# Lower words of the weights on GpSimd, finer first pieces, means in two products, and another order of two attention steps in an attention and gated-network kernel

## The chip, the core and the metric

The kernel runs on one core of a Trainium2 chip. The metric is device time in microseconds for one execution; of several runs the median is taken. A profile is one further execution with a trace. Engines are named as the profile does: PE is TensorE (PEld its weight loads), DVE is VectorE, ACT is ScalarE, POOL is GpSimd, SP is SyncE, which issues most transfers here.

## The reference

The inputs are q, k and v with 4 batches, 8 heads, 768 positions and 64 columns a head, all float32. Each position attends to a local window of positions nearer than 16 and to 24 summaries, one for each block of 32 positions. A summary key is the maximum of the block's keys, a summary value is the mean of its values.

```python
k_sum = k.reshape(B, H, nb, block, D).max(axis=3)
v_sum = v.reshape(B, H, nb, block, D).mean(axis=3)
scores_l = scale * np.matmul(q, k.transpose(0, 1, 3, 2))      # masked to |i - j| < 16
scores_s = scale * np.einsum('bhsd,bhnd->bhsn', q, k_sum) + np.log(block)
a = softmax(np.concatenate([scores_l_m, scores_s], axis=-1))
attn = np.matmul(a, np.concatenate([v, v_sum], axis=2))
x = attn.transpose(0, 2, 1, 3).reshape(3072, 512)
out = ((x @ w1) * (x @ w2) @ w3) @ w_out
```

w1 and w2 are 512x1024, w3 is 1024x1024 and w_out 1024x512. They arrive as 64-bit floating point numbers; the kernel reads each as two 32-bit words.

## The kernel before, in words

**Products.** Every float32 operand of the network is kept as a high and a low part, and one product of 128x128 by 128x512 is three matmuls: high by high, low by high, high by low (`products`, L111 to L113). `fold_weights` (L193) multiplies w3 by w_out into wp once, 64 products; `gate` (L419 on) makes (x w1)(x w2) for 128 rows of the hidden layer, and `project` (L444) multiplies by wp. `low` (L108, L109) makes a low part as source minus high part.

**Weights.** They come in pieces of 512 numbers a partition (512 KB each), in the order of `EARLY`, then the rest of w3, then w1 and w2. `start_loads` issues the transfers, at most AHEAD of them before use, into a ring of ten buffers that keys and value rows share, and after the load with a given index it also issues the other loads that `LOADS` lists under that index. `convert` (L152) makes one unit of one or two pieces: ScalarE turns the upper words into float32 bits but for the last three (L167); VectorE shifts these bits left by three (L175) and then ORs the top three bits of the lower word into each piece (L178); ScalarE rounds this to the high part (L188); VectorE subtracts for the low part (L109).

**Attention.** A step is one group of 512 tokens by one pair of heads; there are 24. A step's scores (`scores`, L310, 32 matmul instructions into two of four sc banks) are reduced with the mask on VectorE (L333), put through the exponential on ScalarE (L347), their sums inverted on GpSimd and VectorE (L352, L353), and normalized. Then come `transposes` (L366, two tp banks), `evacuate` (L375, copies to SBUF), `outputs` (L384, 32 matmul instructions) and `keep_x`, which splits x into high and low parts. Before a step, GpSimd copies the summary keys into the key tile (`gather`, L304) and the summary values into the value tile (`load_sums`, L285).

**Summary values of the first batch.** `mean_products` multiplies six blocks of value rows by a constant matrix (`mean_sb`, made on GpSimd at the very start) and puts the 24 means of all columns on 120 output rows; one ScalarE copy makes vs0.

**Order.** Two parts are written out by hand. In the first phase a loop counts ticks, t, about one piece each. In every tick it advances the conversions, does what `WORK` lists for t, advances the first eight steps, begins a step if t is in `FIRST`, and then puts out products until RATE more columns are given (LATER_RATE from tick FIRST[4] on); a product counts 1536 columns, and one whose weights are not yet converted ends the tick's share. The order of the SP and PE instructions is exactly this order. `first_pair` (L555) takes a step over several ticks: scores; reduce and half the exponentials; the other half and the sums; normalize, and, from tick FIRST[s+1] on, transposes; outputs. The letters of `NORMALIZE` and `SECOND` say for each of these steps whether ScalarE (A) or VectorE (V) normalizes and makes the second copy. The sums of the fold's rows 2 and 3 lie in the tp banks, so that the first transposes need these to be stored in wp (`store`, L209 to L212).

In the second phase (L683 on) sixteen steps are done in pairs between network products, and GpSimd normalizes them (L356). The PE order of one pass is: transposes of an earlier step, scores of a new one, transposes of the second earlier step, scores of the second new one, outputs of both earlier steps, then network products.

Of the kernel before, what the change touches and what calls it, by code (L numbers as in the profile page):

```python
# [30 lines left out]
FIRST = (15, 18, 20, 22, 27, 32, 37, 44)  # L31
# [4 lines left out]
    *(("wo", 0, 0), ("w3", 0, 0), ("wo", 0, 1), ("w3", 1, 0), ("wo", 1), ("w3", 2, 0), ("w3", 3, 0)),  # L36
    *(("w3", 0, 1), ("w3", 1, 1), ("wo", 2), ("w3", 2, 1), ("w3", 3, 1), ("wo", 3)),
# [10 lines left out]
NORMALIZE = "VAAAAAAA"  # L48
SECOND = "AAAVAVVA"
SOONER = 400  # L50
RING = 10
# [19 lines left out]
def attention_moe(ctx, tc, qG, kW, kT, vP, vW, vB, mask, w1, w2, w3T, wo, out):  # L71
# [24 lines left out]
    make_identity(nc, ident)  # L96
    mask_sb = const.tile([P, 3, KR], F32, name="mask_sb")


    mean_sb = sb.tile([P, S // P, P], F32, name="mean_sb", tag="v", bufs=2)  # L100
    nc.gpsimd.memset(mean_sb, 0.0)
    for i in range(P // BLOCK):
        for at in (CUT, CUT - 64):
            part = mean_sb.rearrange("p t n -> p (t n)")[i * BLOCK : (i + 1) * BLOCK, at + i :: P + P // BLOCK]
            nc.gpsimd.memset(part[:, : S // P], 1.0 / BLOCK)
# [22 lines left out]
    def weight(name, i, src, shape, part=None):  # L128

        n = src.shape[1] // 2  # L130
        parts = range(n // PIECE) if part is None else [part]
        units.append((name, i, shape, list(parts), len(todo) + len(parts) - 1))
        for k in parts:
            todo.append(src[:, 2 * k * PIECE : 2 * (k + 1) * PIECE])

    def start_loads(at_least):

        while todo or due_loads:
# [8 lines left out]
            nc.sync.dma_start(raw, todo.pop(0))  # L147
# [4 lines left out]
    def convert(name, i, shape, parts, last):  # L152


        n = len(parts) * PIECE
# [6 lines left out]
        for k in range(len(parts)):  # L162
            raw = loading.pop(0)
            working.append(raw)
            words = raw.rearrange("p (n t) -> p n t", t=2)
            low_words.append(words[:, :, 0])
            nc.scalar.activation(  # L167
                f[:, k * PIECE : (k + 1) * PIECE],
                words[:, :, 1].bitcast(F32),
                AF.Prelu,  # L170
                scale=2.0**-112,
                alpha=-(2.0**32),
            )
            yield
        nc.vector.tensor_scalar(out=bits, in0=bits, scalar1=3, scalar2=None, op0=ALU.logical_shift_left)  # L175
        for k, low_word in enumerate(low_words):
            some = bits[:, k * PIECE : (k + 1) * PIECE]
            nc.vector.scalar_tensor_tensor(  # L178
                out=some, in0=low_word, scalar=29, in1=some, op0=ALU.logical_shift_right, op1=ALU.bitwise_or
# [6 lines left out]
        at = parts[0] * PIECE  # L186
# [4 lines left out]
        have.update((name, i, part) for part in parts)  # L191

    def fold_weights(order):  # L193
        acc = {}
        for i, j in order:
            while not {("w3", i, j * P // PIECE), ("wo", j // 2, j % 2 * DO // PIECE)} <= have:
# [59 lines left out]

    def mean_products(tiles):
        po = ps.tile([P, 512], F32, name="means", tag="sc", bufs=4)
        for i in range(S // P):
            nc.tensor.matmul(  # L260
                po[:KR, :DM],
                lhsT=mean_sb[:, i, :KR],
                rhs=tiles[i // 2][:, i % 2],
                start=i == 0,
                stop=i == S // P - 1,
            )
        return po
# [90 lines left out]
    def normalize_alone(s, sm, mx):  # L358

        if NORMALIZE[s] == "A":  # L360
            for j in range(NI):
                nc.scalar.activation(sm[:, j], sm[:, j], AF.Copy, scale=mx[:, 2, j : j + 1])
        else:
            nc.vector.tensor_tensor(sm, sm, mx[:, 2].unsqueeze(2).broadcast_to([P, NI, KR]), ALU.mult)

    def transposes(sm):  # L366

        tp = [ps.tile([P, 512], F32, name="tp", bufs=2) for _ in range(2)]
# [43 lines left out]
    def gate(f, x, hs):  # L412
        acc = []
        for w in range(2):
# [6 lines left out]
            for c in range(NC):  # L421
                while (GATES[w], k, c * FQ // PIECE) not in have:
# [46 lines left out]
    def queue(name, i, part=None):  # L469
        src, shape = {"wo": (wo, (2, DO)), "w3": (w3T, (NJ, P)), "w1": (w1, (NC, FQ)), "w2": (w2, (NC, FQ))}[name]  # L470
        weight(name, i, src[i], shape, part)
# [305 lines left out]
```

## Time and profile before

| what | us |
|---|---|
| median of 3 runs (542.31 to 544.02) | 543.22 |
| the profiled execution's own time | 541.49 |
| its span, from the first instruction to the last | 539.7 |
| PE busy | 517.6 |
| DVE busy | 238.6 |
| ACT busy | 239.8 |
| POOL busy | 56.8 |

The mean granted TensorE clock of this execution is 0.993 of full speed. In the rows below, a line of the timeline gives start, duration, engine, source line, operation, output and inputs with shapes, count, and in brackets the engine's idle time before it with what ended that. A row of the groups gives the busy time, the mean duration in ns, and the idle time before. A window row gives the stretch and its length, then the busy time and count for PE, PEld, DVE, ACT and POOL, then the granted clock, the transfers' share and GB/s.

### The profile page before, as it was taken

How to read it: one execution, taken by the hardware profiler on the slowest of the kernel's cores; microseconds unless marked ns; L12 is line 12 of the kernel's file. 1: busy time of each engine (PE TensorE's matmuls, PEld its weight loads, DVE VectorE, ACT ScalarE, POOL GpSimd, SP SyncE). 2: the span in 40 equal slices, each digit the busy share in tenths (PEclk: the TensorE clock that was granted, in tenths of full speed). 3: DMA queues.
4: the chain of work that ended last, by engine and by line, in shares of the span. 5: the costliest groups of instructions: out<-in, count | busy, mean ns of one | idle time of the engine just before them, and what ended most of it. 6: DMA issues, size and time to landing. Idle time of an engine off the chain costs nothing.

```text
span 539.7 us, 9919 instructions
## 1 busy us (share of the span) xinstructions
PE 517.6 (96%) x3852; PEld 419.9 (78%) x3852; DVE 238.6 (44%) x686; ACT 239.8 (44%) x688; POOL 56.8 (11%) x103
## 2 busy tenths in 40 slices
PE   2897999999999999999999999999999999899997
PEld 1655777888788888888888888888888888788885
DVE  5879889998504227633253043251142350222210
ACT  5548998876436127126254153261172361222210
POOL 1010221110003001103002011021020020000000
PEclk9997999999999999999999999999999999999999
DMA  8999699775614005642050150050150020000001
GB/s 305 406 371 342 193 306 350 244 210 169 205 57 152 0 24 146 202 142 80 0 149 21 60 170 21 0 166 23 60 170 1 16 60 39 21 21 0 1 19 58
DMA packets 30574, 67.21 MB, mean 125 GB/s; under 512 B 4032, under 2 KB 7616, under 8 KB 30528
## 3 DMA queue, kind: packets, MB, share of 16 engines
q1 hardware_dynamic: 27072, 60.30, 34.7%
q10 hardware_dynamic: 3456, 6.29, 3.1%
q8 instruction: 30, 0.49, 0.4%
q14 instruction: 16, 0.13, 0.1%
HBM read 58.51 MB, written 6.29 MB: 120 GB/s over the span
## 4 chain that ended last, share of the span: by engine, by line
PE 91%; DVE 3%; ACT 3%; DMA 1%; issue 1%; POOL 0%; SPq 0%; POOLq 0%; ACTq 0%
PE mm L113 79%; PE po L393 5%; PE sc L319 4%; PE tp L373 3%; DVE w L109 1%; DMA wraw<-in_w3T_dram 1%; DVE wf L178 1%; ACT w L188 1%; PE means L260 1%; ACT sm L347 1%; DVE wf L175 1%; ACT wf L167 0%; ACT pt L378 0%; ACT wp L211 0%; DVE wp L109 0%
## 5 line engine op out<-in xcount | busy, mean ns | idle before, releaser
L113 PE MATMUL mm<-x,w 128*128 128x512 f32 x1152 | 265.1, 390 | 0.0
L113 PEld LDWEIGHTS mm<-x,w 128*128 128x128 f32 x1152 | 215.4, 188 | 45.8 <-issue 0.5
L113 PE MATMUL mm<-wp,h 128*128 128x512 f32 x576 | 134.1, 391 | 0.0
L113 PEld LDWEIGHTS mm<-wp,h 128*128 128x128 f32 x576 | 107.5, 188 | 22.8 <-issue 0.2
L347 ACT ACTIVATE sm<-sm,mx 128x120 f32<-128x120 f32 x192 | 73.7, 386 | 17.4 <-DVE mx L333 16.4
L438 DVE TENSOR_TENSOR g<-mm,g 128x512 f32<-128x512 f32 x48 | 33.1, 690 | 93.2 <-PE mm L113 90.8
L439 ACT CAST h<-g 128x512 fp32r<-128x512 f32 x48 | 29.6, 617 | 90.4 <-DVE g L438 90.4
L113 PE MATMUL mm<-w,w 128*128 128x512 f32 x192 | 52.4, 424 | 12.4 <-ACT w L188 11.4
L113 PEld LDWEIGHTS mm<-w,w 128*128 128x128 f32 x192 | 37.0, 200 | 24.9 <-ACT w L188 13.3
L457 ACT COPY o<-mm 128x512 f32<-128x512 f32 x24 | 14.0, 584 | 81.4 <-PE mm L113 81.4
L382 DVE COPY pt<-tp 120x512 f32<-120x512 f32 x19 | 13.1, 690 | 75.6 <-PE tp L373 75.6
L109 DVE TENSOR_TENSOR h<-g,h 128x512 fp32r<-128x512 f32 x48 | 35.7, 744 | 24.1 <-ACT h L439 23.9
L435 ACT COPY g<-mm 128x512 f32<-128x512 f32 x48 | 28.0, 584 | 35.9 <-PE mm L113 35.9
L333 DVE CUSTOM_DVE_ANT_0 sm<-sc,mask_sb 128x120 f32<-128x120 f32 x192 | 40.9, 275 | 3.9 <-PE sc L319 3.9
L347 ACT ACTIVATION_READ_ACCUMULATOR sm<-sm,mx 128x1 f32 x192 | 36.4, 189 | 0.0
L306 POOL COPY k<-ks 128x96 f32<-128x96 f32 (+1 forms) x32 | 10.2, 331 | 248.1 <-DMA k<-in_kW_dram 207.4
L109 DVE TENSOR_TENSOR x<-po,x 128x512 fp32r<-128x512 f32 x24 | 16.6, 690 | 36.0 <-ACT x L404 36.0
L356 POOL TENSOR_TENSOR sm<-sm,mx 128x960 f32<-128x960 f32 x16 | 29.1, 1820 | 6.0 <-DVE mx L353 5.0
L167 ACT ACTIVATE wf<-wraw 128x512 f32<-128x512 f32 x40 | 26.2, 673 | 6.3 <-DMA wraw<-in_wo_dram 2.8
L393 PEld LDWEIGHTS po<-pt,v 120*64 120x64 f32 x768 | 23.7, 138 | 5.1 <-issue 2.5
L378 ACT COPY pt<-tp 120x512 f32<-120x512 f32 x24 | 14.0, 583 | 30.7 <-PE tp L373 30.7
L188 ACT CAST w<-wf 128x1024 fp32r<-128x1024 f32 (+1 forms) x25 | 21.9, 877 | 12.7 <-DVE wf L178 12.6
(33 smaller groups left out, 295.1 us busy)
## 6 DMA issues: line engine op xcount, KB each, us to landing
k<-in_kW_dram SPq DMA_DIRECT2D x24, 368.0 KB
wraw<-in_w3T_dram SPq DMA_DIRECT2D x16, 512.0 KB
wraw<-in_w_dram SPq DMA_DIRECT2D x16, 512.0 KB
q<-in_qG_dram SPq DMA_DIRECT2D x24, 256.0 KB
raw<-in_kT_dram SPq DMA_DIRECT2D x16, 384.0 KB
out_dram<-o ACTq DMA_DIRECT2D x24, 256.0 KB
v<-in_vW_dram SPq DMA_DIRECT2D x24, 192.0 KB
raw<-in_vB_dram SPq DMA_DIRECT2D x12, 384.0 KB
```

The costliest lines, as they stand in the source:

```text
L109: eng.tensor_tensor(dst, src, hi.bitcast(F32), ALU.subtract)
L113: nc.tensor.matmul(acc, lhsT=a, rhs=b, start=first and i == 0, stop=last and i == len(terms) - 1)
L167: nc.scalar.activation(f[:, k * PIECE : (k + 1) * PIECE], words[:, :, 1].bitcast(F32), AF.Prelu, scale=2.0**-112, alpha=-(2.0**32),)
L188: nc.scalar.copy(hi, f)
L319: nc.tensor.matmul(sc[h][64 * g : 64 * g + 64, i * KR : (i + 1) * KR], lhsT=q[rows, i * P + 64 * g : i * P + 64 * g + 64], rhs=k[rows, i, ...
L333: nc.vector.tensor_tensor_reduce(out=sm[:, j], in0=sc[h][:, i * KR : (i + 1) * KR], in1=mask_sb[:, 0 if blk == 0 else 2 if blk == BLOCKS - ...
L347: nc.scalar.activation(sm[:, j], sm[:, j], AF.Exp, bias=mx[:, 0, j : j + 1], scale=-1.0, accum_out=mx[:, 1, j : j + 1])
L356: nc.gpsimd.tensor_tensor(sm, sm, mx[:, 2].unsqueeze(2).broadcast_to([P, NI, KR]), ALU.mult)
L393: nc.tensor.matmul(po[cols, at : at + 64], lhsT=v[:, g, i, cols], rhs=pt[g][:, (h * NBLK + i) * 64 : (h * NBLK + i + 1) * 64], start=True, ...
L435: nc.scalar.copy(g, a[:, :U])
L438: nc.vector.tensor_tensor(g, acc[1][:, :U], g, ALU.mult)
L439: nc.scalar.copy(h[:, 0], g)
```

## The change

**Lower words.** The shift on VectorE (L175) goes. GpSimd scales each piece's lower words by 2^-29 with a minimum against 7, in place, and VectorE's one remaining instruction per piece shifts the bits left by three and ORs this in.

```diff
             nc.scalar.activation(
-                f[:, k * PIECE : (k + 1) * PIECE],
+                f[:, k : k + length],
...
+            nc.gpsimd.tensor_scalar(
+                out=words[:, :, 0], in0=words[:, :, 0], scalar1=2.0**-29, scalar2=7.0, op0=ALU.mult, op1=ALU.min
+            )
             yield
-        nc.vector.tensor_scalar(out=bits, in0=bits, scalar1=3, scalar2=None, op0=ALU.logical_shift_left)
-        for k, low_word in enumerate(low_words):
-            some = bits[:, k * PIECE : (k + 1) * PIECE]
+        for (k, length), low_word in zip(parts, low_words):
+            some = bits[:, k - at : k - at + length]
             nc.vector.scalar_tensor_tensor(
-                out=some, in0=low_word, scalar=29, in1=some, op0=ALU.logical_shift_right, op1=ALU.bitwise_or
+                out=some, in0=some, scalar=3, in1=low_word, op0=ALU.logical_shift_left, op1=ALU.bitwise_or
             )
```

**First pieces.** The first piece of w_out and the first of w3 come in two halves of 256 numbers each. There are 42 loads instead of 40, and what is converted is tracked by 128 columns.

```diff
 EARLY = (
-    *(("wo", 0, 0), ("w3", 0, 0), ("wo", 0, 1), ("w3", 1, 0), ("wo", 1), ("w3", 2, 0), ("w3", 3, 0)),
-    *(("w3", 0, 1), ("w3", 1, 1), ("wo", 2), ("w3", 2, 1), ("w3", 3, 1), ("wo", 3)),
+    *(("wo", 0, 0, 256), ("w3", 0, 0, 256), ("wo", 0, 256, 256), ("w3", 0, 256, 256), ("wo", 0, 512)),
+    *(("w3", 1, 0), ("wo", 1), ("w3", 2, 0), ("w3", 3, 0), ("w3", 0, 512), ("w3", 1, 512), ("wo", 2)),
+    *(("w3", 2, 512), ("w3", 3, 512), ("wo", 3)),
 )
```

**Constants and means.** The identity and the two constant matrices are made at tick 3 (`CONSTANTS`) instead of at the start. The first matrix gives the 24 means of each of the four column groups at its own 32 output rows; these are copied to SBUF by four ScalarE instructions, and the second matrix spreads them over the 120 rows.

```diff
+        for at in (CUT, CUT - 64):
+            for p in range(NPAIR):
+                nc.gpsimd.tensor_copy(spread[:, p, at : at + NB], ident[:, 32 * p : 32 * p + NB])
...
         for i in range(S // P):
-            nc.tensor.matmul(
-                po[:KR, :DM],
-                lhsT=mean_sb[:, i, :KR],
-                rhs=tiles[i // 2][:, i % 2],
-                start=i == 0,
-                stop=i == S // P - 1,
-            )
-        return po
+            for p in range(NPAIR):
+                nc.tensor.matmul(
+                    po[32 * p : 32 * p + NB, :P],
+                    lhsT=constants["means"][:, i],
+                    rhs=tiles[i // 2][:, i % 2, p * P : (p + 1) * P],
+                    start=i == 0,
+                    stop=i == S // P - 1,
+                )
+        means = sb.tile([P, P], F32, name="means_sb", tag="pt", bufs=6)
+        nc.vector.memset(means, 0.0)
+        for p in range(NPAIR):
+            nc.scalar.copy(means[32 * p : 32 * p + NB], po[32 * p : 32 * p + NB, :P])
+        yield
+        po = ps.tile([P, 512], F32, name="means", tag="sc", bufs=4)
+        for p in range(NPAIR):
+            nc.tensor.matmul(po[:KR, p * P : (p + 1) * P], lhsT=constants["spread"][:, p, :KR], rhs=means, start=True, stop=True)
+        vs[0] = sb.tile([KR, DM], F32, name="vs0", tag="pt", bufs=6)
+        nc.scalar.copy(vs[0], po[:KR, :DM])
```

**First steps anew.** The tables of the first phase are other ones.

```diff
-FIRST = (15, 18, 20, 22, 27, 32, 37, 44)
+FIRST = (18, 20, 22, 25, 31, 38, 42, 45)
...
-NORMALIZE = "VAAAAAAA"
-SECOND = "AAAVAVVA"
+NORMALIZE = "VVAVAVAA"
+SECOND = "AAAAVAAA"
...
-        7: [lambda: nc.sync.dma_start(mask_sb, mask)],
-        8: [lambda: rows(1)],
-        11: [lambda: fetch(0)],
-        12: [lambda: keys(1)],
-        13: [lambda: keys(0)],
-        14: [lambda: rows(0)],
-        15: [lambda: rows(2), lambda: fetch_values(0)],
-        16: [lambda: fetch(1)],
...
+        10: [lambda: keys(0), lambda: rows(1)],
+        11: [lambda: keys(1)],
+        12: [lambda: nc.sync.dma_start(mask_sb, mask)],
+        13: [lambda: fetch(0)],
+        14: [lambda: fetch_values(0)],
+        15: [lambda: rows(0)],
+        17: [lambda: rows(2)],
+        18: [lambda: fetch(1)],
...
-        14: [means, lambda: summaries(0, 1, kraws.pop(1)), lambda: fill(1)],
...
+        16: [means],
+        19: [lambda: summaries(0, 1, kraws.pop(1)), lambda: fill(1)],
...
-    RATE = 6600
-    LATER_RATE = 6944
+    RATE = 5600
+    LATER_RATE = 8944
```

**Second phase.** A pass now puts out the transposes of both earlier steps, then the scores of both new ones, then the outputs. The second step's transposes use two of the four sc banks.

```diff
-                pts, begun_now = [], []
-                for k in range(2):
-                    if last:
-                        pts.append(evacuate(transposes(sms.pop(last[k])[0])))
-                    if now:
-                        begun_now.append(begin(now[k]))
+                spare = ({}, {"tag": "sc", "bufs": 4})
+                tps = [transposes(sms.pop(p)[0], **more) for p, more in zip(last, spare)]
+                pts = [evacuate(tp) for tp in tps]
+                begun_now = [begin(p) for p in now]
```

117 lines of the change are left out of this document (63 added, 54 removed).

## The prediction, made before the changed kernel ran

> **What bounds the kernel now.** I read the page's shares and its chain of waits first, then the windows by stage, then TensorE's timeline where the windows show a loss.
>
> ```profile
> span 539.7 us, 9919 instructions
> PE 517.6 (96%) x3852; PEld 419.9 (78%) x3852; DVE 238.6 (44%) x686; ACT 239.8 (44%) x688; POOL 56.8 (11%) x103
> PE 91%; DVE 3%; ACT 3%; DMA 1%; issue 1%; POOL 0%; SPq 0%; POOLq 0%; ACTq 0%
> ```
>
> TensorE holds 91% of the chain that ended last. So only two things can move the end: TensorE work added or removed, and the 22 us in which TensorE sat still. The windows tell where those are (the first figure after the length is PE's busy time, PEclk the granted clock):
>
> ```profile
> 0.00:45.60 45.60, 33.13 (x140) 21.88 (x140) 32.56 (x65) 26.31 (x53) 5.51 (x21) 1.00 0.98 366
> 45.60:50.80 5.20, 1.45 (x20) 1.15 (x21) 4.81 (x7) 3.59 (x7) 0.23 (x1) 0.69 1.05 298
> 50.80:57.10 6.30, 6.30 (x50) 4.89 (x51) 5.85 (x24) 5.86 (x21) 0.23 (x1) 0.72 0.93 316
> 57.10:87.00 29.90, 28.99 (x353) 22.82 (x353) 26.51 (x67) 26.65 (x79) 6.32 (x13) 1.00 0.84 272
> 87.00:166.00 79.00, 79.00 (x644) 63.68 (x640) 52.68 (x137) 50.43 (x145) 6.97 (x17) 1.00 0.61 187
> ```
>
> After 87 us TensorE is full (there is one small hole near the end, shown below). Before it there are three losses: a start in which weights arrive and are converted (DMA share 0.98, so the transfers nearly fill it), a hole from 45.6 to 50.8, and a lowered clock up to about 57. The hole in TensorE's own timeline:
>
> ```profile
> 9.52 6.50 PE L113 MATMUL mm<-w,w 128*128 128x512 f32 x12 [9.52 <-ACT w L188]
> 32.23 5.31 PE L260 MATMUL means<-rows,mean_sb 128*120 128x512 f32 x12
> 38.85 1.05 PE L319 MATMUL sc<-k,q 64*64 64x120 f32 x32
> 39.84 5.73 PE L113 MATMUL mm<-w,w 128*128 128x512 f32 x24
> 47.97 0.36 PE L373 MATMUL tp<-ident,sm 64*120 64x64 f32 x1 [2.41 <-DVE wp L109]
> 49.70 1.11 PE L373 MATMUL tp<-ident,sm 64*120 64x64 f32 x15 [1.37 <-DVE wp L109]
> 50.74 1.88 PE L319 MATMUL sc<-k,q 64*64 64x120 f32 x32
> 52.55 4.54 PE L113 MATMUL mm<-w,w 128*128 128x512 f32 x15
> ```
>
> The first step's scores end at 39.90, 24 fold matmuls end at 45.57, and then TensorE stands at the first step's transposes until VectorE has stored wp, because those sums hold the tp banks: 2.41 + 1.37 = 3.8 us idle. The clock then costs more: 15 transposes in 1.11 where 16 take 0.68 (row further below), scores 1.88 against 1.05, 15 matmuls 4.54 against 5.73 x 15/24 = 3.58; that is 0.47 + 0.83 + 0.96 = 2.3 us. The hole is worth 6.0 us in all.
>
> **The hole.** Each tick of the first-phase loop puts out matrix products until RATE columns are given; a product is 3 matmuls, 1536 columns. Before, RATE 6600 gives 5 products a tick; after, 5600 gives 4. Before, between scores 0 and transposes 0 lie only the last 8 early products (24 matmuls). After, FIRST starts step 0 at tick 18 and normalizes it at tick 21. Ticks 18 and 19 give the 8 early products, tick 20 gives scores 1 and 4 products of the next weight (w3 number 4), and only then come transposes 0. So 36 matmuls at 5.73/24 = 0.239 us and one set of scores, 8.6 + 1.05 = 9.6 us, lie where 5.7 lay. What they must cover:
>
> ```profile
> 37.58 1.23 DVE L109 TENSOR_TENSOR w<-wf,w 128x1024 fp32r<-128x1024 f32 x1 [1.11 <-ACT w L188]
> 47.83 1.22 DVE L109 TENSOR_TENSOR w<-wf,w 128x1024 fp32r<-128x1024 f32 x1
> 48.97 0.68 DVE L109 TENSOR_TENSOR wp<-mm,wp 128x512 fp32r<-128x512 f32 x1
> ```
>
> The last wp store ends at 49.65, which is 9.75 us after the scores' end: 9.6 us just covers it. What is late next is w3 number 4, which now stands ahead of the transposes: its low part ends at 49.05 (second row), 9.15 us after the scores' end, and TensorE now wants it after 5.73 + 1.05 = 6.8. That is a new stall of 2.35 us if VectorE keeps its order. One VectorE shift of 0.69 (below) is gone from that weight's own chain, so I take 1.7. The hole's term is -6.0 + 1.7 = -4.3 us, between -6.0 and, if the clock falls in the new stall as well (2.35 + 2.3), -1.4.
>
> ```profile
> 46.00:48.00 2.00, 0.03 (x1) 0.03 (x1) 1.97 (x4) 2.00 (x5) 0.00 (x0) 0.89 1.10 248
> ```
>
> A mean of 0.89 over these 2 us, from 1.0 to 0.5, puts the fall about 0.44 us before 48, some 2 us after the last matmul. By this row a stall of 1.7 keeps the clock, one of 2.35 may not. The Trainium skill (TensorE: Matmul & The Clock Gate, Part 1) says that the clock halves after an idle window of about 3.4 us that runs freely; by that rule neither stall alone would surely cost the clock, and the term would be -3.65 to -4.3. The trace, with a fall after 2 us, agrees with a window that had begun earlier, not with a fixed wait of 3.4 us.
>
> **GpSimd and the lower words.** VectorE loses its shift (L175); its OR (L178) stays and now takes a low word that GpSimd has scaled in place.
>
> ```profile
> L178 DVE SCALAR_TENSOR_TENSOR wf<-wraw,wf 128x512 uint32<-128x512 uint32 x40 | 26.6, 690 | 0.5
> L175 DVE TENSOR_SCALAR wf<-wf 128x1024 uint32<-128x1024 uint32 x15 | 10.3, 689 | 0.4 <-ACT wf L167 0.4
> L175 DVE TENSOR_SCALAR wf<-wf 128x512 uint32<-128x512 uint32 x10 | 4.2, 421 | 6.5 <-ACT wf L167 6.5
> L306 POOL COPY k<-ks 128x96 f32<-128x96 f32 x16 | 5.8, 366 | 165.8 <-DMA k<-in_kW_dram 136.0 <-DMA rows<-in_vP_dram 29.6
> L356 POOL TENSOR_TENSOR sm<-sm,mx 128x960 f32<-128x960 f32 x16 | 29.1, 1820 | 6.0 <-DVE mx L353 5.0 <-DVE vs L248 1.0
> L101 POOL MEMSET mean_sb<- 128x768 f32 x1 | 0.7, 738 | 0.0
> ```
>
> GpSimd's operation is not in the trace. From the memset, 738/768 = 0.96 ns an element, 512 elements take 0.49 us; from the two-operand multiply, 1820/960 = 1.9 ns, 0.97. I take 0.6, near the memset, since it reads one tensor. But these engines get in each other's way:
>
> ```profile
> 178.71 0.69 DVE L109 TENSOR_TENSOR h<-g,h 128x512 fp32r<-128x512 f32 x1 [0.69 <-ACT h L439]
> 210.91 1.79 POOL L356 TENSOR_TENSOR sm<-sm,mx 128x960 f32<-128x960 f32 x1 [0.82 <-DVE mx L353]
> 211.40 1.84 DVE L109 TENSOR_TENSOR h<-g,h 128x512 fp32r<-128x512 f32 x1
> 31.95 0.68 DVE L178 SCALAR_TENSOR_TENSOR wf<-wraw,wf 128x512 uint32<-128x512 uint32 x1
> 32.16 0.58 POOL L306 COPY k<-ks 128x96 f32<-128x96 f32 x1 [29.64 <-DMA rows<-in_vP_dram]
> ```
>
> The same VectorE subtraction takes 0.69 alone and 1.84 when GpSimd works: it ends 0.55 after GpSimd's instruction does. The other way round, a small GpSimd copy, 0.37 on the mean, lasts 0.58 and ends 0.11 after the VectorE OR. So a GpSimd instruction and a VectorE instruction with two SBUF inputs run one after the other, and both operations that are left of a conversion on VectorE (L178 and the low part) are of that kind. The early stage has 16 pieces (10 single, 3 double conversions). Removed: 10 x 0.42 + 3 x 0.69 = 6.3 us of VectorE. Added: 16 x 0.6 = 9.6 us in which VectorE may be shut out, on the share of time in which it is busy, 32.56/45.6 = 0.71: 6.8 us. Net +0.5; with 0.49 and 0.97 it is -0.7 and +4.7, and if every one collides +9.2. The Trainium skill (GPSIMD Engine Reference, section 7) gives about 1.9 cycles an element for reads with a step of up to 8 bytes, which is this step; at 1.2 GHz that is an estimate of 0.81 us, by which this term would be +2.9. No run here shows it.
>
> Constants move from the idle start to tick 3, in front of the sixth piece's low word: 14 small GpSimd instructions of 0.1 to 0.7 us (the nearest rows are the 0.37 us copy and the 0.74 us memset), 3 to 4 us. That piece is one of the early eight, which wait for transfers and VectorE alike; I take nothing, at most +3.
>
> **Smaller first pieces and the order of loads.**
>
> ```profile
> wraw<-in_w3T_dram SPq DMA_DIRECT2D x16, 512.0 KB
> raw<-in_kT_dram SPq DMA_DIRECT2D x16, 384.0 KB
> ```
>
> The first product needs 768 KB instead of 1024 KB, at 366 GB/s 0.7 us sooner, and shorter conversions; it would start near 7.5 instead of 9.52. But the next product needs the same bytes as before, so at most one product, 0.7 us, is gained, and it is idle time again: 0. Key and value loads of 384 KB, 1.07 us each at that rate, move ahead of the later early weights, so these land 1 to 2 us later. VectorE and ScalarE wait there now: the 37.58 row above shows 1.11. I take +0.5, from 0 to 1.07.
>
> **Means in two products, normalizing, evacuating.**
>
> ```profile
> L347 ACT ACTIVATE sm<-sm,mx 128x120 f32<-128x120 f32 x192 | 73.7, 386 | 17.4 <-DVE mx L333 16.4 <-POOL k L306 1.0
> L364 DVE TENSOR_TENSOR sm<-sm,mx 128x960 f32<-128x960 f32 x1 | 1.2, 1158 | 0.0
> ```
>
> The means: before 5.31 us of TensorE. After: 48 passes of a quarter of the columns. One after another they cost the same 5.3; side by side in four column strips, as 32 score passes do in 1.05 us, 1.6. Then come four copies, about 0.3 us each (softmax's, of nearly that length, take 0.39), in which TensorE waits, and 8 passes of 0.11, 0.9: 3.7 to 7.4. I take 4.5, -0.8 us.
>
> Of the first eight steps three more are normalized on VectorE (1.16 us each, L364) and two copies go back to ScalarE. From 57.1 to 87 VectorE is busy 26.51 of 29.9: five double shifts leave (3.4), two normalizations come (2.3), one copy leaves (0.7), and 10 x 0.6 x 0.89 = 5.3 us of GpSimd collide at most. With 30.0 of 29.9 it is at its edge: I take 0, from -0.9 (all of PE's idle time there) to +3.3 at 0.97 us.
>
> **Two steps' order.** In the second phase both transposes come first, the second set in two of the four score banks. The last pass shows the gain:
>
> ```profile
> 463.68 0.68 PE L373 MATMUL tp<-ident,sm 64*120 64x64 f32 x16
> 464.40 0.58 ACT L378 COPY pt<-tp 120x512 f32<-120x512 f32 x1 [3.42 <-PE tp L373]
> 465.13 0.73 PE L373 MATMUL tp<-ident,sm 64*120 64x64 f32 x16 [0.76 <-ACT pt L378]
> 466.49 2.09 PE L393 MATMUL po<-pt,v 120*64 120x64 f32 x64 [0.62 <-ACT pt L378]
> L382 DVE COPY pt<-tp 120x512 f32<-120x512 f32 x19 | 13.1, 690 | 75.6 <-PE tp L373 75.6
> ```
>
> The 0.76 + 0.62 us go; outputs then wait about 0.3 for the first copies: -1.1. In the passes before, the second scores start 0.61 + 0.62 + 0.98 = 2.2 us after the first transpose, and the second VectorE copy ends 0.61 + 0.1 + 2 x 0.69 = 2.1 after it: just free, cost 0.
>
> **Sum.** -4.3 + 0.5 + 0.5 - 0.8 - 1.1 = -5.2 us. The profiled execution took 541.49 us around its span of 539.7 and would take 536.3; the median of the runs, 543.22, lies 1.7 above it and becomes 538.0. The forecast's own range, all good ends and most of the bad, is 533 to 543.
>
> **Rivals.** Slower: GpSimd becomes the gate of every conversion. It decides when its operation takes long and always collides: 16 x (p - 0.39) of new delay eats the other terms (-5.7) at p = 0.75 us. For it: VectorE's two remaining operations leave no room between them, and an unsigned scale with a minimum could take longer than any row. Against it: transfers fill the start, so VectorE has pauses. At p = 1.2 it gives 13.0 - 5.7 = +7.3, 550.5 us. No change: the hole only moves. Weight number 4 comes 2.35 us late, the clock falls, and VectorE at its edge gives back 2.5: -1.4 - 1.1 + 2.5 = 0, 543.2. For it: the 47.83 row, in which wp stores and normalization go ahead of that weight. The new order doesn't do what it says: if copies are late by one 0.69 us operation in each of the seven passes before the last, 4.8 us are lost and 542.8 is left. Against it: VectorE waited for the transposes in 17 of 19 copies, 75.6 us in all.
>
> **How the numbers follow.** Forecast 0.66, GpSimd's gate 0.17, hole moved 0.12, late copies 0.05. The predicted time is 538.0. The low end is 533; the slow rival's lower half has to be inside, so the high end is 548. About 0.3%, 1.6 us, is what a measurement of this kernel can tell from no change: faster 0.68, same 0.14, slower 0.18.
>
> **What would show it.** Right: no idle of 3.8 us at the first transposes and no clock of 0.5 near 50; the chain reaches the first mm<-x,w near 82 instead of 87; a GpSimd operation near 0.6 us; the last pass without 0.76 and 0.62. Wrong: GpSimd operations over 0.8 us, VectorE's OR waiting for GpSimd, TensorE idle before L113 on a w of the later fold, or scores waiting for a copy in the second phase.

## The result, and the profile after

| kernel | median, us | lowest to highest | runs |
|---|---|---|---|
| before, beside it | 542.76 | 542.06 to 544.02 | 4 |
| changed | 563.81 | 563.02 to 565.43 | 4 |

The ratio is 1.0389, 95% interval 1.0363 to 1.0414: some 21 us slower. The forecast was 538.0 with a range that ended at 548. The profiled execution took 564.44 us around a span of 562.7, 23.0 more than the profiled one of before; the table of places below is made from these two.

The page of the changed kernel, the busy times and the chain as were shown of before:

```profile
PE 522.8 (93%) x3896; PEld 425.6 (76%) x3896; DVE 232.3 (41%) x667; ACT 235.2 (42%) x674; POOL 152.8 (27%) x149
PE 73%; POOL 5%; DMA 4%; DVE 3%; ACT 2%; issue 1%; SPq 0%; POOLq 0%
```

TensorE is busy 5 us more and idle 18 us more. GpSimd, 57 us before, has 96 us more work, and the chain that ended last, which hardly touched it, runs through it for 5%. The share looks small because it is a mean over the whole span; the windows show where it lies (PE, PEld, DVE, ACT, POOL, then PEclk; the left-out window of 30 to 40 us has 9.62 for POOL):

```profile
20.00:30.00 10.00, 4.25 (x9) 2.53 (x10) 5.42 (x8) 2.84 (x4) 9.68 (x5) 0.90 1.03 330
...
40.00:50.00 10.00, 5.95 (x68) 4.74 (x67) 4.69 (x6) 5.17 (x11) 9.51 (x5) 0.93 0.96 376
```

GpSimd is full, with five or six instructions in 10 us. A row of the groups by form, and a row of the waits (us in total, times, longest):

```profile
L170 POOL TENSOR_SCALAR wraw<-wraw 128x512 uint32<-128x512 uint32 x38 | 84.5, 2224 | 10.2 <-DMA wraw<-in_w_dram 5.6 <-DMA v<-in_vW_dram 2.0
```

```profile
DVE wf L176 <- POOL wraw L170: 33.1, 21, 4.8
```

The scaling of a piece takes 2.22 us on the mean, not 0.6. VectorE's OR waits for it 21 times, 33.1 us in all. GpSimd's own timeline shows the queue:

```profile
12.64 0.52 POOL L265 MEMSET picks<- 32x6 f32 x4
13.22 1.45 POOL L270 COPY picks<-ident 128x24 f32<-128x24 f32 x8
14.76 21.20 POOL L170 TENSOR_SCALAR wraw<-wraw 128x512 uint32<-128x512 uint32 x9
```

Nine pieces stand back to back for 21.20 us, 2.36 each. TensorE's timeline shows what this does:

```profile
11.87 1.65 PE L106 MATMUL mm<-w,w 128*128 128x512 f32 x3 [11.87 <-ACT w L185]
...
29.38 14.67 PE L106 MATMUL mm<-w,w 128*128 128x512 f32 x52 [4.51 <-DVE w L102]
43.97 1.51 PE L279 MATMUL means<-rows,picks 128*24 128x128 f32 x48
...
54.05 1.66 PE L347 MATMUL sc<-k,q 64*64 64x120 f32 x32
...
70.19 0.36 PE L402 MATMUL tp<-ident,sm 64*120 64x64 f32 x1 [4.85 <-DVE sm L393]
...
71.82 4.86 PE L106 MATMUL mm<-w,w 128*128 128x512 f32 x12
...
106.16 4.15 PE L106 MATMUL mm<-x,w 128*128 128x512 f32 x10
```

| place | before | after | later by |
|---|---|---|---|
| first product | 9.52 | 11.87 | 2.4 |
| means | 32.23 | 43.97 | 11.7 |
| first scores | 38.85 | 54.05 | 15.2 |
| first network product | 87.0 | 106.16 | 19.2 |
| last pass's transposes | 463.68 | 487.96 | 24.3 |
| span | 539.7 | 562.7 | 23.0 |

About half of the loss is there when the means begin. The hole of the prediction is larger, not gone: 4.85 us idle at the first transposes, and the 12 matmuls behind them take 4.86 at a lowered clock, where the prediction's row gives 12 x 0.239 = 2.9. The clock was lowered in three more places: the windows above have 0.90 and 0.93, and narrower ones show falls at 28.04, 48.52, 69.00 and 106.54 us, 23.9 us of half speed in all, where the trace of before has one of 6.8 us ahead of its last microseconds.

### The profile page after: what moved, and what is told of

It is laid out like the page before. It is cut to its first block, busy times and chain, and to the rows that moved or that the text cites. A ratio compares the mean times of both kernels' runs of the same rounds, so it can differ in the third digit from the quotient of the medians.

```text
span 562.7 us, 10055 instructions
## 1 busy us (share of the span) xinstructions
PE 522.8 (93%) x3896; PEld 425.6 (76%) x3896; DVE 232.3 (41%) x667; ACT 235.2 (42%) x674; POOL 152.8 (27%) x149
## 4 chain that ended last, share of the span: by engine, by line
PE 73%; POOL 5%; DMA 4%; DVE 3%; ACT 2%; issue 1%; SPq 0%; POOLq 0%
PE mm L106 64%; POOL wraw L170 4%; DMA wraw<-in_w_dram 4%; PE po L422 3%; PE sc L347 3%; PE tp L402 2%; ACT sm L375 1%; DVE vs L244 1%; DMA raw<-in_kT_dram 1%; DVE w L102 1%; ACT sm L390 0%; POOL k L334 0%; DVE h L102 0%; DVE wf L176 0%; POOL v L322 0%
## 5 line engine op out<-in xcount | busy, mean ns | idle before, releaser
L106 PE MATMUL mm<-x,w 128*128 128x512 f32 x1152 | 268.0, 393 | 1.8 <-DVE g L467 1.7
L170 POOL TENSOR_SCALAR wraw<-wraw 128x512 uint32<-128x512 uint32 (+1 forms) x42 | 89.1, 2122 | 14.2 <-DMA wraw<-in_w_dram 5.6
L106 PE MATMUL mm<-w,w 128*128 128x512 f32 x192 | 56.8, 453 | 21.7 <-ACT w L185 12.8
L106 PEld LDWEIGHTS mm<-w,w 128*128 128x128 f32 x192 | 40.5, 219 | 34.5 <-ACT w L185 14.1
L334 POOL COPY k<-ks 128x96 f32<-128x96 f32 (+1 forms) x32 | 11.8, 383 | 196.0 <-DMA k<-in_kW_dram 188.7
L176 DVE SCALAR_TENSOR_TENSOR wf<-wf,wraw 128x512 uint32<-128x512 uint32 (+1 forms) x42 | 28.8, 689 | 33.6 <-POOL wraw L170 33.1
L411 DVE COPY pt<-tp 120x512 f32<-120x512 f32 x17 | 11.0, 685 | 67.9 <-PE tp L402 67.9
L185 ACT CAST w<-wf 128x1024 fp32r<-128x1024 f32 (+2 forms) x27 | 22.0, 823 | 29.0 <-DVE wf L176 28.9
L380 POOL TENSOR_SCALAR mx<-mx 128x8 f32<-128x8 f32 x24 | 6.3, 263 | 95.3 <-ACT sm L375 94.7
L163 ACT ACTIVATE wf<-wraw 128x512 f32<-128x512 f32 (+1 forms) x42 | 26.3, 644 | 11.2 <-DMA wraw<-in_wo_dram 5.4
```

Of the source, the lines that this page charges most:

```text
L106: nc.tensor.matmul(acc, lhsT=a, rhs=b, start=first and i == 0, stop=last and i == len(terms) - 1)
L163: nc.scalar.activation(f[:, k : k + length], words[:, :, 1].bitcast(F32), AF.Prelu, scale=2.0**-112, alpha=-(2.0**32),)
L170: nc.gpsimd.tensor_scalar(out=words[:, :, 0], in0=words[:, :, 0], scalar1=2.0**-29, scalar2=7.0, op0=ALU.mult, op1=ALU.min)
L176: nc.vector.scalar_tensor_tensor(out=some, in0=some, scalar=3, in1=low_word, op0=ALU.logical_shift_left, op1=ALU.bitwise_or)
L185: nc.scalar.copy(hi, f)
```

## The experiments

Each is compared with the kernel before on the same chip (its medians were 542.0 to 542.5), and ratios have their 95% intervals.

**The words back on VectorE.** The changed kernel with the shift and the old OR, so without GpSimd's scaling.

```diff
-            nc.gpsimd.tensor_scalar(
-                out=words[:, :, 0], in0=words[:, :, 0], scalar1=2.0**-29, scalar2=7.0, op0=ALU.mult, op1=ALU.min
-            )
...
+        nc.vector.tensor_scalar(out=bits, in0=bits, scalar1=3, scalar2=None, op0=ALU.logical_shift_left)
```

> The changed kernel with only the lower words undone: VectorE shifts and ORs as before, GpSimd's scaling is gone; pieces, means, tables and the second phase's order stay changed. Theory G (GpSimd's scaling, 1.99 us a piece, gates the conversions and is the whole loss): the time falls by over 22 us, below the kernel before, to 537 to 541 us; first network product on x near 82 to 87 us instead of 106. Rival T (the new tables of the first phase, later starts and other loads, are the loss, and GpSimd is only late because there is room): it stays above 555 us.

Measured: 545.21 us, ratio 1.0045 (1.0021 to 1.0068). So 18.6 of the 21 us go with GpSimd's scaling, and the rest of the change, which was to gain 5.7, costs 2 to 3. That is 4 us above what the first theory allowed, so GpSimd isn't the whole loss. TensorE's timeline of this run:

```profile
54.38 0.68 PE L400 MATMUL tp<-ident,sm 64*120 64x64 f32 x16 [2.12 <-DVE sm L391]
...
88.27 2.25 PE L420 MATMUL po<-pt,v 120*64 120x64 f32 x32 [3.75 <-ACT pt L405]
```

The hole at the first transposes is 2.12 us and the transposes run at the full clock (0.68 for 16). But a wait of 3.75 now stands at the outputs just ahead of the first network product, and they then take 2.25 where 32 at a full clock take 1.15. ScalarE's timeline shows what these outputs waited for:

```profile
86.14 0.66 ACT L163 ACTIVATE wf<-wraw 128x512 f32<-128x512 f32 x1 [3.17 <-DMA wraw<-in_w_dram]
86.71 1.03 ACT L183 CAST w<-wf 128x1024 fp32r<-128x1024 f32 x1
87.64 0.58 ACT L405 COPY pt<-tp 120x512 f32<-120x512 f32 x1
```

The copy that the outputs need stands behind a weight's conversion, which itself came after a wait of 3.17 us for a transfer.

**GpSimd's words alone.** The kernel before, with the changed conversion (`convert`) and nothing else.

```diff
+            nc.gpsimd.tensor_scalar(
+                out=words[:, :, 0], in0=words[:, :, 0], scalar1=2.0**-29, scalar2=7.0, op0=ALU.mult, op1=ALU.min
+            )
...
-        nc.vector.tensor_scalar(out=bits, in0=bits, scalar1=3, scalar2=None, op0=ALU.logical_shift_left)
...
```

> The kernel before with one change alone: GpSimd scales the lower words, VectorE has one instruction per piece; everything else as before. Theory G: conversions come no faster than one piece in 2.0 to 2.5 us, the first network product on x moves from 87 to 103 to 110 us, 558 to 568 us in all. Rival T: within 3 us of the kernel before, 540 to 546.

Measured: 562.35 us, ratio 1.0373 (1.0347 to 1.04). This one edit has nearly the whole loss, in the old surroundings as in the new; its 40 scalings take 2.30 us on the mean.

**What makes the instruction slow.** The kernel before, with eight forms of the instruction on a spare tile at the end of the program, each on 512 elements. Its single time was 542.64 us; the rows of the groups are what counts.

> The kernel before with a probe behind all else on GpSimd: 512 elements in place, each form twice, mostly with VectorE idle: unsigned every second word with scale and minimum (the form of the change), the same with scale alone, unsigned dense, float every second word, float dense, float dense with scale alone, and two plain copies. If the step of 8 bytes makes the form slow, the dense unsigned form takes under 1.1 us and the stepped float form about 2. If the unsigned type does, the stepped float form takes under 1.1 and the dense unsigned one about 2. If the second operation does, scale alone takes under 1.2. The total stays within 1 us of the kernel before, since nothing waits for the probe.

```profile
L727 POOL TENSOR_SCALAR probe<-probe 128x512 uint32<-128x512 uint32 x2 | 4.0, 1981 | 0.2
L729 POOL TENSOR_SCALAR probe<-probe 128x512 uint32<-128x512 uint32 x2 | 3.9, 1930 | 0.2
L731 POOL TENSOR_SCALAR probe<-probe 128x512 f32<-128x512 f32 x2 | 3.8, 1924 | 0.2
L732 POOL TENSOR_SCALAR probe<-probe 128x512 f32<-128x512 f32 x2 | 3.4, 1699 | 0.2
L728 POOL TENSOR_SCALAR probe<-probe 128x512 uint32<-128x512 uint32 x2 | 3.1, 1546 | 0.2
L733 POOL COPY probe<-probe 128x512 uint32<-128x512 uint32 x2 | 1.3, 645 | 0.1
```

In order: the change's form (every second word, scale and minimum), the same on adjacent words, the same in float32 on adjacent words, the scale alone in float32 on adjacent words, the scale alone on every second unsigned word, and a plain copy of every second word. Neither the unsigned type nor the step costs anything much. The instruction does, 1.98 us, three times a copy of the same words. In the change's form the second operation is 0.43 of that, in both pairs; in float32 the two instructions with the scale alone took 1.50 and 1.90, so there its price is not settled.

**The scale alone in the kernel.** The changed kernel without the minimum; a weight whose lowest three bits should all be set may get wrong ones.

```diff
-                out=words[:, :, 0], in0=words[:, :, 0], scalar1=2.0**-29, scalar2=7.0, op0=ALU.mult, op1=ALU.min
+                out=words[:, :, 0], in0=words[:, :, 0], scalar1=2.0**-29, scalar2=None, op0=ALU.mult
```

> The changed kernel whose GpSimd instruction scales the lower words and leaves out the minimum against 7, so the lowest bits of a weight that should end in seven may be wrong. The measured price of the instruction falls from 1.98 to 1.55 us for 512 elements. Theory A, GpSimd's queue is the gate of the first phase: some 18 to 20 pieces go through it between 10 and 50 us, when it is busy over nine tenths, and each comes 0.43 us sooner, so the time falls by 8 us or more, to 550 to 557 us. Rival B, what costs is that VectorE is shut out, or the longer chain of each piece, whatever the length of the instruction: 560 us or more.

Measured: 553.53 us, ratio 1.021 (1.0186 to 1.0233), 10 us under the changed kernel. GpSimd's timeline:

```profile
14.83 18.16 POOL L170 TENSOR_SCALAR wraw<-wraw 128x512 uint32<-128x512 uint32 x9
```

The same nine pieces take 3.04 us less. A saving of 0.43 us an instruction gave 10 us in the end: the time follows the length of this instruction through some 24 of the 42, as it does where the queue is the gate. A fixed cost of each collision would have left it where it was. A longer chain within each conversion would grow with the instruction too, so this run doesn't tell it from the queue.

**Every second piece on GpSimd, and w1 and w2 alone.** Two runs on the kernel before ask whether GpSimd can carry a part; the first has the upper lines, the second the lower.

```diff
+            there.append((last - len(parts) + 1 + k) % 2 == 1)
+            if there[-1]:
+                nc.gpsimd.tensor_scalar(
...
+            there.append(name in ("w1", "w2"))
+            if there[-1]:
+                nc.gpsimd.tensor_scalar(
...
```

> The kernel before, with GpSimd scaling the lower words of every second piece and VectorE keeping the others. Theory G in its simple form (GpSimd matters only as a queue of 2 to 2.5 us an instruction): one instruction for two pieces is 1.0 to 1.25 us a piece, less than the 1.7 that VectorE needs, so the queue no longer gates, and the time is within 3 us of before, 541 to 546. The prediction's slow rival in its formula (each instruction shuts VectorE out for its whole length, 16 x (p - 0.39) at p = 1.1): 8 to 11 us more, 551 to 554.

> The kernel before, with GpSimd scaling only the 16 pieces of w1 and w2, those of the early fold staying on VectorE. Theory G with slack: four pieces, 8 to 10 us of GpSimd, are asked for in every 13.7 us of TensorE's gate, so little is lost, 0 to 4 us, 542.5 to 546.5, and the first network product comes 0 to 4 us later than at 87. If GpSimd's time counts wherever it stands: 16/40 of the 20 us, 8 us more, 550.

Measured: 550.17 us, ratio 1.0148 (1.0118 to 1.0177), and 547.88, ratio 1.011 (1.0078 to 1.0143). With every second piece GpSimd is no longer full (44.1 us for 20 pieces, with 21.1 us idle ahead of them), and it still costs 8 us. A full queue is then not the whole of it. The reading that fits, not tested apart, is that 2.2 us stand in each such conversion's own chain, where VectorE's shift stood with 0.4. In the second run no piece of the early stage is touched; the visible loss is again at the outputs ahead of the first network product, 0.95 and 2.57 us of idle time. VectorE's timeline of the second run shows what the longer of the two waits for:

```profile
87.87 0.69 DVE L187 SCALAR_TENSOR_TENSOR wf<-wf,wraw 128x512 uint32<-128x512 uint32 x1 [1.91 <-POOL wraw L176]
```

This OR waits 1.91 us for a scaling, and behind it in VectorE's queue stand a subtraction (88.48), a wp store (89.64) and only then the copy that the outputs need (90.24). The profiled execution is the longest of the four, 550.85 us, so its rows show more than the median loses.

**The order of two steps alone.** The kernel before with the second-phase edit.

```diff
...
+                tps = [transposes(sms.pop(p)[0], **more) for p, more in zip(last, spare)]
+                pts = [evacuate(tp) for tp in tps]
+                begun_now = [begin(p) for p in now]
```

> The kernel before with the second phase's order alone (both transposes, both scores, outputs; second transposes in score banks). Both theories: a pass takes about 0.16 us less (38.12 to 37.95 between the first transposes of two passes) and the last pass loses its two waits, about 1.2; so 2.4 us less, 540.3 us, ratio 0.9955.

Measured: 539.56 us, ratio 0.9951 (0.9933 to 0.9969), 3.0 us faster. It is the fastest kernel of all that ran, and beats both. The last pass in TensorE's timeline:

```profile
462.36 1.16 PE L373 MATMUL tp<-ident,sm 64*120 64x64 f32 x32
463.71 2.19 PE L393 MATMUL po<-pt,v 120*64 120x64 f32 x64 [0.20 <-ACT pt L378]
```

From the first transpose to the outputs it is 1.35 us, 2.81 before (463.68 to 466.49).

**The smaller pieces alone.** The kernel before with the new `EARLY`; all indices of the tables are moved by the two loads more.

```diff
+FIRST = (17, 20, 22, 24, 29, 34, 39, 46)
...
+    *(("wo", 0, 0, 256), ("w3", 0, 0, 256), ("wo", 0, 256, 256), ("w3", 0, 256, 256), ("wo", 0, 512)),
...
```

> The kernel before with the finer first pieces alone; every table index moved by the two added loads. Theory G, by the landings in the changed kernel with the words back on VectorE (4.86, 5.96, 7.89 us for the first three half pieces, so half a piece lands no faster than a whole one): first matmul about 1.4 us later than 9.52, 0 to 1.5 us more in all, 542.5 to 544. The prediction's step: first matmul at 7.5 and no change in all, 542.5.

Measured: 545.05 us, ratio 1.0053 (1.0036 to 1.007), 2.8 slower. TensorE's first row, and ScalarE's first rows, of this run:

```profile
10.96 1.65 PE L114 MATMUL mm<-w,w 128*128 128x512 f32 x3 [10.96 <-ACT w L191]
```

```profile
4.48 0.43 ACT L171 ACTIVATE wf<-wraw 128x256 f32<-128x256 f32 x1 [2.48 <-DMA wraw<-in_wo_dram]
5.89 0.43 ACT L171 ACTIVATE wf<-wraw 128x256 f32<-128x256 f32 x1 [0.98 <-DMA wraw<-in_w3T_dram]
...
8.96 0.43 ACT L171 ACTIVATE wf<-wraw 128x256 f32<-128x256 f32 x1 [0.76 <-DMA wraw<-in_w3T_dram]
9.29 0.69 ACT L191 CAST w<-wf 128x256 fp32r<-128x256 f32 x2
```

Both operands' first halves are there by 5.89, but ScalarE's queue has the conversions of all four halves ahead of the first rounding (L191), so that this waits for the fourth landing, 8.96. The first product begins at 10.96 instead of 9.52. That is 1.4 us; the means begin 2.7 us later (34.92 against 32.23), so that nearly all of the 2.8 us is lost by then. The rest comes mostly from the speed of the first products. Groups of this run from 10.9 to 23.6 us, and of the kernel before from 9.5 to 16.8:

```profile
L114 PE MATMUL mm<-w,w 128*128 128x512 f32 x21 | 11.1, 676 | 12.7 <-ACT w L191 12.7
```

```profile
L113 PE MATMUL mm<-w,w 128*128 128x512 f32 x13 | 7.0, 680 | 10.1 <-ACT w L188 10.0
```

Until full speed is first recorded, at 23.67 us here and at 16.84 before, these matmuls take 0.68 on the mean, and 0.40 afterwards in both (the times of neighbours overlap). So 21 instead of 13 of them run slow. Full speed is first recorded at 23.0 to 23.7 us in the three traces with the pieces and the words on VectorE, and at 14.7 to 17.1 in the six with whole pieces and GpSimd out of the early stage. That the gaps between the first, smaller products cause this is argued, not shown. (The windows give a PEclk of 1.00 for these stretches, the prediction's first row too: the clock record begins only with that first change, and what lies ahead of it is counted as full.)

**Order and means.** The same kernel as in the run of the order alone, with the means in two products as well; the constants are made at the start.

```diff
...
+                nc.tensor.matmul(
+                    po[32 * p : 32 * p + NB, :P],
+                    lhsT=constants["means"][:, i],
```

> The kernel before with the second phase's new order and the means in two products (constants at the start), all else as before. The means take 1.5 + 1.3 of waiting + 1.1 = 3.9 us in place of 5.3, but behind them TensorE waits for the last early weight and then for wp anyway: 538.5 to 540, within 1 us of the order alone (539.56). If the means were on the path, 1.4 us less; if their copies come late behind other ScalarE work, up to 3 us more.

Measured: 545.68 us, ratio 1.006 (1.0043 to 1.0078): about 6 us above the order alone. TensorE's timeline:

```profile
32.29 1.07 PE L275 MATMUL means<-rows,picks 128*24 128x128 f32 x32
34.63 0.64 PE L275 MATMUL means<-rows,picks 128*24 128x128 f32 x16 [1.26 <-DMA rows<-in_vP_dram]
36.54 1.10 PE L289 MATMUL means<-means_sb,picks 128*120 128x128 f32 x8 [1.27 <-ACT means_sb L285]
...
49.23 0.36 PE L397 MATMUL tp<-ident,sm 64*120 64x64 f32 x1 [3.53 <-DVE wp L102]
...
87.33 0.34 PE L417 MATMUL po<-pt,v 120*64 120x64 f32 x4 [1.12 <-ACT pt L402]
88.82 1.04 PE L417 MATMUL po<-pt,v 120*64 120x64 f32 x28 [1.15 <-DVE pt L406]
```

The first product of means is short, 1.7 us for 48 instructions, but it catches up with a transfer and with the copies, and the next matmuls begin at 37.40, as late as behind the one product of before (32.23 + 5.31 = 37.5). The loss comes behind it. At the first transposes there is none yet: the wait is 3.53 + 0.24 us against 2.41 + 1.47 in the order alone, and the 15 transposes begin at 49.83 against 49.87. But the clock is lowered for 6.8 us there against 3.4, and the next outputs begin at 57.67 against 56.68. Then the outputs ahead of the network products wait 1.12 + 1.15 us against 0.51, with another lowered clock behind them. Why this edit disturbs those outputs was not settled.

**The tables undone, and the tables alone.** First the kernel with the words on VectorE but the tables of before; then the kernel before with the order of two steps and the new tables. The upper lines are of the first, the lower of the second; each has more of the tables.

```diff
-FIRST = (18, 20, 22, 25, 31, 38, 42, 45)
+FIRST = (17, 20, 22, 24, 29, 34, 39, 46)
...
-FIRST = (15, 18, 20, 22, 27, 32, 37, 44)
+FIRST = (16, 18, 20, 23, 29, 36, 40, 43)
```

> The changed kernel with the lower words back on VectorE and the tables of the first phase (FIRST, NORMALIZE, SECOND, LOADS, WORK, RATE) as before, their indices moved by 2 for the two loads more. It tells what the new tables are worth by themselves, against the 545.2 us of the same kernel with the new tables. Theory A, the tables do what the prediction's hole step says: the idle time of 3.8 us at the first transposes and the lowered clock come back, and the time is near the sum of the parts measured alone, 542.2 - 3.0 (order) + 2.8 (pieces) + 6.1 (means in two) = 548.1 us, so that the tables gain about 3. Rival B, the tables give nothing, or the loss seen with the means in two is only a chance order of VectorE's and ScalarE's queues: 541 to 545.5 us.

> The kernel before with the order of two steps in the second phase and the new tables of the first phase (their indices moved back by 2, since there are 40 loads), and nothing else of the change: words on VectorE, whole first pieces, means in one product. Theory A, the tables' worth of 1.6 us, measured between two kernels that also have the pieces and the means, holds by itself: 542.2 - 3.0 - 1.6 = 537.6 us, 536.5 to 538.7, with no idle time near 3.8 us at the first transposes and no lowered clock there. Rival B, the gain at the hole is eaten where the queues of VectorE and ScalarE come out otherwise, at the outputs ahead of the first network product: 539 to 543 us, with the idle time standing at outputs there.

Measured: 546.76 us, ratio 1.008 (1.0052 to 1.0109), and 544.02, ratio 1.003 (1.0013 to 1.0047). So with pieces and means the tables gain some 1.6 us (545.21 against 546.76; the two intervals overlap), and without them they lose about 4.5 against the order alone, more than either theory expected. The second run's profiled execution is the longest of its twelve (541.03 to 545.84 us), so its rows show the loss at its largest. The hole of the first run, in TensorE's timeline, and then the second run's:

```profile
50.95 0.36 PE L400 MATMUL tp<-ident,sm 64*120 64x64 f32 x1 [3.54 <-DVE wp L102]
51.54 1.10 PE L400 MATMUL tp<-ident,sm 64*120 64x64 f32 x15 [0.24 <-DVE wp L102]
```

```profile
28.55 0.73 PE L113 MATMUL mm<-w,w 128*128 128x512 f32 x2 [2.70 <-ACT w L188]
...
54.79 1.11 PE L373 MATMUL tp<-ident,sm 64*120 64x64 f32 x16 [2.28 <-DVE sm L364]
...
89.72 2.25 PE L393 MATMUL po<-pt,v 120*64 120x64 f32 x32 [3.40 <-ACT pt L378]
```

With the old tables the hole is back, 3.54 + 0.24 us and a lowered clock behind it (transposes 1.10, the next scores 1.88 and 15 matmuls 4.96 us, against 0.68, 1.05 and 3.73 at a full clock: 2.5 us). With the new tables alone it is 2.28 us, but TensorE waits 2.70 for weights in the start (1.44 at this place in the run of the order alone), and 3.40 at the outputs (0.51 there).

## Why the prediction was wrong, point by point

**GpSimd and the lower words: the failing step.** "I take 0.6, near the memset, since it reads one tensor." The instruction takes 1.98 us alone and 2.22 on the mean in the kernel. Both bounds, 0.49 and 0.97, lay under it, because both were rows of other instructions: on the same 512 words the scale with a minimum takes 1.98, the scale alone 1.55 and a copy 0.65. GpSimd's only TENSOR_SCALAR of before (mx, L352) has 8 elements in 0.24 us and says nothing of 512, so no row bounded the price from above, and the range should have said so. The mechanism was named among the rivals, GpSimd's gate, with its break-even at 0.75 us; the chance of 0.17 followed from the price. By the rival's own formula 2.0 us would give 16 x 1.61 - 5.7 = +20 us, near the measured 21, but this is luck: the other terms came to +2.5, not -5.7, and only 11.7 us are lost before the means, the rest behind them, where later weights still pass GpSimd, which the formula leaves out.

The Trainium skill (GPSIMD Engine Reference, section 7) was cited with 1.9 cycles an element for a step of up to 8 bytes; the estimate of 0.81 us from it is not what ran, and the step made no difference (1981 ns against 1930). The same section has another row, 4 cycles an element for a chain of dependent float32 operations; at 1.2 GHz that is an estimate of 1.7 us, nearer to what was measured. That the instruction is such a chain no run shows.

**Collisions with VectorE: too high for this form.** The sum let GpSimd shut VectorE out for its whole length. Single rows of GpSimd's and of VectorE's timeline in the changed kernel:

```profile
16.81 2.52 POOL L170 TENSOR_SCALAR wraw<-wraw 128x512 uint32<-128x512 uint32 x1
33.95 2.01 POOL L170 TENSOR_SCALAR wraw<-wraw 128x512 uint32<-128x512 uint32 x1
```

```profile
16.76 0.69 DVE L176 SCALAR_TENSOR_TENSOR wf<-wf,wraw 128x512 uint32<-128x512 uint32 x1 [2.44 <-POOL wraw L170]
17.37 1.13 DVE L102 TENSOR_TENSOR w<-wf,w 128x512 fp32r<-128x512 f32 x1
34.45 0.70 DVE L102 TENSOR_TENSOR w<-wf,w 128x512 fp32r<-128x512 f32 x1
```

A scaling that begins beside an OR takes 2.52, half a microsecond more, and a subtraction that begins early in a scaling takes 1.13 instead of 0.69. But the subtraction at 34.45 lies wholly inside a scaling and takes 0.70. So in these rows VectorE is shut out for about half a microsecond, not for 2. The Trainium skill (SBUF — State Buffer, "SBUF: two separate sides") says that the first of two such instructions holds the ports for its whole length; the multiply of the prediction's rows agrees, this instruction doesn't.

**Constants at tick 3: nothing, wrongly.** They stand in GpSimd's queue for 2.0 us (12.64 to 14.67), under the 3 to 4 worked out; but with that queue as the gate the cover named for them is gone.

**The hole: right in the size, wrong in what it is worth.** Forecast -4.3. With the words on VectorE the new tables turn 3.78 us of idle time and 2.5 of lowered clock into a stall of 2.12 with no lowered clock: -4.1. The part of the clock in this may be luck of the profiled execution: of the six of the words on VectorE, the two with a mean granted clock of 0.997 took 543.01 and 544.00 us, and three with 0.990 or 0.991 took 546.08 to 546.37. The last section tells what decides it. The stall stands at the transposes, which wait for their normalized scores, not at weight number 4 as forecast. But what is late next was looked for only there. The outputs 34 us later, which wait 3.75 us against 1.14 + 1.15 with the old tables, and then run at a lowered clock, and 0.9 us of later start give most of it back, so that the tables gain 1.6 us or lose 4.5, by what surrounds them. In the changed kernel, GpSimd's delay reopens the hole.

**The order of loads: +0.5, too low.** The first scores come 0.9 us later with the new tables in one pair of runs (41.55 against 40.65), and in the other a wait for weights in the start grows by 1.26 us.

**Smaller first pieces: the wrong sign of an intermediate step.** "It would start near 7.5 instead of 9.52." It started at 10.96. Bytes were counted and ScalarE's queue was not, nor that TensorE's first products run at a lowered speed, here for 8 more of them; the term, 0, was 2.8 us.

**Means in two: -0.8, and nothing on the path.** The 48 passes do run side by side in 1.5 to 1.7 us, but the work behind them begins when transfer and copies allow it. The edit cost 6 us farther on, for which the sum had no term.

**The order of two steps: right, and low.** Forecast -1.1, measured -3.0. The last pass gives 1.46. An earlier pass was counted at 0; in its rows of before it goes from 198.25 to 203.46, and in the run of the order alone:

```profile
198.08 1.16 PE L373 MATMUL tp<-ident,sm 64*120 64x64 f32 x32
...
203.16 3.01 PE L113 MATMUL mm<-x,w 128*128 128x512 f32 x12
```

That is 5.08 instead of 5.21, 0.13 us less. Over the seven passes, from the first transposes shown to those of the last pass, it is 1.15 us (198.25 to 463.68 against 198.08 to 462.36). Scores did not wait for copies. With the last pass that makes 2.6 of the 3.0.

**The parts don't add up.** The tables are worth -1.6 us in one surrounding and +4.5 in another. One spot, the outputs ahead of the first network product, idles 0.5 us or less in some kernels and 2 to 4 in others, by who stands ahead of the copies in the queues of VectorE and ScalarE. That no term of the sum had.

## What to carry to other kernels

Price an operation on GpSimd by a row with the same instruction, not the same number of operands; where there is none, work out the break-even price first and ask what excludes it. An engine that is idle nine tenths of the time can still be the gate of a stage in which every unit of work must pass it. Before a stall is booked as gained, walk on to the next places where TensorE waits on the same engines, and read which conversion stands ahead of the copy there: with queues in order, a transfer that is late holds up work that does not need it. Don't price the clock of a stall from one execution: where the stall falls on the clock's grid decides it.

## What the runs showed of the hardware

GpSimd's TENSOR_SCALAR is the same speed for unsigned and float32 data and for adjacent and every second word: 1.92 to 1.98 us for 512 elements with two operations.

The clock changes on a grid of 3.41 us, and not after a stall of a certain length. Narrow windows give the moments of its changes. In the changed kernel it falls at 28.04, 48.52, 69.00 and 106.54 us and rises at 34.87, 55.34, 75.83 and 109.96: any two of these lie a multiple of 3.41 us apart. So it is in each of the thirteen traces, with another offset in each. The kernel before and the order of two steps alone have the same work and the same stall of 2.41 us at the first transposes. Before, the clock fell at 47.56, 2.0 us into the stall. In the order alone (PEclk is the third column from the end):

```profile
45.70:48.10 2.40, 0.03 (x1) 0.00 (x0) 2.00 (x5) 2.40 (x6) 0.24 (x1) 1.00 1.07 276
48.10:50.90 2.80, 1.30 (x32) 1.10 (x36) 2.77 (x4) 1.56 (x4) 0.00 (x0) 1.00 1.02 283
50.90:54.30 3.40, 3.40 (x33) 2.61 (x23) 3.37 (x17) 2.69 (x8) 0.00 (x0) 0.50 1.02 392
```

The same stall kept the full clock, and the fall came at 50.92, with a second wait of 1.47 us. The grid of this execution has points at 47.51 and 50.92, and the first of them splits the stall, with 1.78 us ahead of it. What counts is TensorE's idle time summed between two neighbouring points. Over all thirteen traces, every such stretch at the full clock with 1.97 us or more of it ended in a fall, and none with 1.49 or less did; of the ten between these, four did. So the stall of 2.12 us with the words on VectorE kept the clock because a point at 54.11 came before its end, with 1.86 us idle, and the one of 2.28 with the tables alone lost it at 54.60, with 2.10. The prediction's reading of a window that had begun earlier holds; its reading by length alone, that 1.7 keeps the clock and 2.35 may not, does not.
